# The start of an attention and expert-layer kernel: one weight unit converted in two parts, copies before weight passes, other banks, tiny products instead of fillers

## The chip, the cores and the metric

The kernel runs on one core of a Trainium2 chip. The metric is the device time of one execution in microseconds; the kernel before has a median of 911.16 us over three runs. The engines are TensorE (PE, with its weight loads PEld), VectorE (DVE), ScalarE (ACT), GpSimd (POOL) and SyncE (SP), which issues nearly all the transfers.

## The reference

Attention over 8 batches of 8 heads, 576 positions of 64 values, each query seeing 32 keys: the last 32 positions in the first four heads, every fourth of the last 128 in the other four. Its output, laid side by side, is the input of a gated layer.

```python
scores = scale * np.matmul(q, k.transpose(0, 1, 3, 2))
...
scores = np.where(masks[None, :, :, :], scores, -1000000000.0)
attn = np.exp(scores - np.max(scores, axis=-1, keepdims=True))
attn = attn / (np.sum(attn, axis=-1, keepdims=True) + 1e-09)
x = np.matmul(attn, v) ...            # 4608 x 512
g = x @ w_gate                        # 512 x 1536
silu = g * (1.0 / (1.0 + np.exp(-g)))
return (silu * (x @ w_val) @ w_out)   # 1536 x 512
```

## The kernel before

**Products.** Every large operand is split into a high part and a low remainder, and a product of two such operands is three products on PE. The weights come as 64-bit numbers and are converted on the chip.

**Attention in packs.** The attention is cut into 40 packs. Pack 0 and 2 hold the first four heads of batch 0 (called plain), packs 1 and 3 the other four (strided); two packs of a kind fill one input chunk of 512 columns. A pack goes through these steps, whose letters stand in the string START: scores on PE (Q), maximum and subtraction on DVE (S), exponential on ACT (X), four transposes on PE (T), a copy out of the bank on ACT or DVE (K, `keys`), results on PE (A), normalising on DVE (N), a transposition on DVE (U), the high copy on ACT (H) and the low difference on POOL or DVE (L; on DVE for the packs in X_LOW). Scores(2), results(3) and so on below name the step of a pack.

**Weights in units.** The weights come in 24 units of 768 columns, each of three thirds of 256. A unit goes through five stages, "ETBHL": exponent on ACT, shift on DVE (or ACT), bits on DVE, high copy on ACT, low difference on POOL (or DVE).

**Order.** START is the order of the first stage, written by hand; q, v and w in it are loads, I and J are filler products into a bank that nobody reads. After it come the items of the layer. The first chunk starts with six items of 256 columns (t = 0 to 5), then items of 512. An item t does its gate products (`bg`, 12 of them), the products of the item before with the output weights (`bo`, 12), and its value products (`bv`, 12). Packs 2 and following are worked in between by `attend(now)`, at the times in EARLY and LATER: a visit "A" does results of pack m-1 and scores of pack m, "B" transposes and copies, "C" the high and low copies. On PE everything runs in the order in which it is written; for the other engines the class Desk sorts the recorded instructions by a cost model that starts at the times in FREE (PE, DVE, ACT, POOL, SP, in ns).

**Banks.** `two` is a pair of banks for scores and results; fs0 and fs1 are pairs for the scores of packs 0 and 1; fk and fx take the transposes of packs 0 and 1, and the fillers.

Of the kernel before, what the change touches and what calls it, by code (L numbers as in the profile page):

```python
# [10 lines left out]
F32 = mybir.dt.float32  # L11
F32R = mybir.dt.float32r
I32 = mybir.dt.int32
# [5 lines left out]
P = 128  # L19
# [41 lines left out]
HALVED = 3  # L61
WARM = 9
TURNED = 20
FREE = 16000, 19500, 17500, 18000, 6000
EARLY = (-1, 1, None), (2, 4, 3), (5, 8, 6)
MASKED = 6
X_LOW, W_LOW, H_LOW, KEYS = (3, 7), (1, 5), (5,), (2,)
ON_ACT = (2, 3, 4, 5, 6, 9, 11, 12, 15, 17, 19, 21, 23)
START = ("q0 q1 w v0 v1 w Q0 Q1 S0 X0 T0 W0 I3 I2 S1 K0 X1 W1 A0 W2 T1 J2 K1 W3 J2 N0 W0 w U0 q2 v2 A1 q3 w w r W4 H0 "
         "L0 N1 U1 H1 L1 W1 v3 W2 W3 W4")  # L70
LATER = (14, 3, 2), (23, 3, 4), (29, 7, 4), (39, 3, 2)
T0 = NPLAIN * CH
NB = S * 8 // CH - 1
# [253 lines left out]
def attention_moe(ctx, tc, qkb, vb, w, const, out):  # L327
# [83 lines left out]
    def w_load(parts=2):  # L411
        nonlocal loaded
        u = loaded
        n = u % 5 if u < NU - NLAST else (u - NU + NLAST) % NRAW
        if u >= NU or raw_of.get(n, -1) >= done["B" if u < NU - 1 else "L"]:
            return False
        raw_of[n] = u
        loaded += 1
        t = at(raw_at[n], 2 * WU, I32)
        n = 2 * WU // parts  # L420
        for k in range(parts):
            nc.sync.dma_start(out=t[:, n * k:n * k + n], in_=w[u // 2, u % 2].bitcast(I32)[:, n * k:n * k + n])
        t = t.rearrange("p (n t) -> p n t", t=2)
        wst[u] = {"lo": t[:, :, 0], "hi": t[:, :, 1]}
        return True

    def w_exp(u):  # L430
        y = wst[u]["hi"].bitcast(F32)
        nc.scalar.activation(out=y, in_=y, func=AF.Prelu, scale=2.0 ** -112, alpha=2.0 ** 32)
# [58 lines left out]
    def w_one(c):  # L491
        u = done[c]
        done[c] += 1
        if c == "E":
            w_exp(u)
        elif c == "T":
            w_shift(u)
        elif c == "B":
            w_bits(u)
        elif c == "H":  # L500
            w_split_hi(u)
        else:
            w_split_lo(u)
        if c in "BL":
            while ready["w"] and w_load():
                pass
# [40 lines left out]
    def masks_of(m, i):  # L547
        n = BK * (pk(m).mask + i * pk(m).mask_step)
        return mask_sb[:, n:n + BK * NG].rearrange("q (g k) -> q g k", g=NG)[:, :, 1:]

    def scores(m, two, masked):

        t = st[m]["qk"]
        if masked:
            for i in range(2):
                nc.tensor.matmul(out=two[:, i, SA:].rearrange("q (g k) -> q g k", g=NG), lhsT=ident16,
                                 rhs=masks_of(m, i), start=True, stop=False, skip_group_check=True)
        for g in range(NG):
            for j in range(NH):
                for i in range(2):  # L560
                    r, q, k = slice(D * i, D * i + D), pk(m).q_at(g, j), pk(m).k_at(i, g, j)
                    nc.tensor.matmul(out=two[BQ * j:BQ * j + BQ, i, SA + BU * g:SA + BU * g + BU],
                                     lhsT=t[r, q:q + BQ], rhs=t[r, k + 1:k + BK], start=not masked,
                                     stop=not masked or g == NG - 1, skip_group_check=True)

    def clear_e(pool):

# [56 lines left out]
    def results(m, two):  # L624

        t, v = st[m]["pt"], st[m]["v"]
        for n in range(NH * NG):
            g, j = divmod(n, NH)
            for i in range(2):
                r = slice(D * i, D * i + D)  # L630
                nc.tensor.matmul(out=two[BQ * j:BQ * j + BQ, i, (D + 1) * g:(D + 1) * (g + 1)],
                                 lhsT=t[r, BQ * at_n(m, n):BQ * at_n(m, n) + BQ], rhs=v[r, n, :], start=True, stop=True,
                                 skip_group_check=True)

    def norm(m, two, pool):
        z = pool["bz"](2 * NG).rearrange("q (i g) -> q i g", i=2)
        y = pool["y"]()
        s = two[:, :, :NG * (D + 1)].rearrange("q i (g c) -> q i g c", g=NG)
        nc.vector.tensor_scalar(out=z, in0=s[:, :, :, D], scalar1=EPS, scalar2=None, op0=ALU.add)
        nc.vector.reciprocal(out=z, in_=z)  # L640
        nc.vector.tensor_tensor(out=y.rearrange("q (c i g d) -> q i g c d", c=2, i=2, g=NG),
                                in0=s[:, :, :, :D].rearrange("q i g (c d) -> q i g c d", c=2),
                                in1=z.unsqueeze(3).unsqueeze(4).broadcast_to([P, 2, NG, 2, D // 2]), op=ALU.mult)
        st[m]["y"] = y
# [148 lines left out]
    def bank(stack, name, n, side="left"):  # L793
        pool = stack.enter_context(tc.tile_pool(name="p" + name, bufs=1, space=bass.MemoryType.PSUM, side=side,
                                                reuse_waits="tile"))
        return pool.tile([P, 512] if n == 1 else [P, n, 512], F32, name=name)

    two = bank_r = bank(ctx, "two", 2)
    k_bank = [bank(of_turns, x, 1, "right") for x in ("fk", "fx")] * 2
    s_banks = [bank(of_scores, x, 2) for x in ("fs0", "fs1")]  # L800

    nc.scalar.dma_start(out=const_sb, in_=const)
    nc.vector.memset(ones, 1.0)
# [10 lines left out]
    def idle(n, bank=k_bank[1]):  # L814

        while n > 0:
            k = min(n, 4)
            nc.tensor.matmul(out=bank[:D, :P * k].rearrange("p (a b) -> p a b", b=D), lhsT=ones,
                             rhs=ones.unsqueeze(1).broadcast_to([P, 2 * k, D]), start=True, stop=True)
            n -= k  # L820

    idle(WARM)

    items = [Item(0, f, a, a + CH // 2) for a in (0, CH // 2) for f in range(HALVED)]
# [2 lines left out]
    first = {  # L827
        "Q": lambda m: scores(m, s_banks[m], True), "S": lambda m: shift(m, s_banks[m], fa, True),
        "X": exps, "T": lambda m: turn_e(m, k_bank[m]), "K": lambda m: keys(m, k_bank[m], fa),
        "A": lambda m: results(m, bank_r), "N": lambda m: norm(m, bank_r, fa),  # L830
        "U": turn_y, "H": lambda m: x_copy(m, "hi"), "L": lambda m: x_copy(m, "lo"),
        "q": lambda m: load_qk(m, fa, nc.sync, 2),
        "v": lambda m: load_v(m, fa, nc.sync, 2),
        "w": lambda m: w_load(3), "r": lambda m: ready.update(w=True), "I": lambda n: idle(n), "J": lambda n: idle(n, k_bank[0]), "W": lambda n: w_one(STAGES[n]),
    }

    et = mybir.EngineType
# [39 lines left out]
    def attend(now):  # L877
        for what, m in visit.get(now, ()):
            r = ended(m)
            if what == "A":  # L880
                if r is not None:
                    results(r, two)
                if m < NPK:
                    scores(m, two, m < MASKED)
                if r is not None:
                    norm(r, two, pool_of(r))
                if m < NPK:
                    shift(m, two, pool_of(m), m < MASKED)
                if r is not None:
                    turn_y(r)  # L890
                if m < NPK:
                    exps(m)
                if 2 * NSTART <= m < TURNED:
                    load_v(m, later, nc.sync)
                elif TURNED <= m - 1 < NPK:
                    load_far(m - 1, later)
                    load_v(m - 1, later, nc.sync)
                if 2 * NSTART <= m + 1 < NPK:
                    load_qk(m + 1, later, nc.sync)
            elif what == "B":  # L900
                if TURNED <= m < NPK:
                    turn_far(m, later)
                elif m < NPK:
                    turn_e(m, two[:, 1])
                    keys(m, two[:, 1], pool_of(m))
            elif r is not None:
                x_copies(r)

# [226 lines left out]
    for t, it in enumerate(items):  # L1135
        before = items[t - 1] if t else None
        late = t >= HALVED
        if it.ci == 0:
            units(it.f)
        gv_mm(it, 0)  # L1140
        act_tanh(it)
        dve_u(it)
        attend(3 * t)
        mixing(t, 0)
        if not late and t:
            out_mm(before, False)
        gv_mm(it, 1)
        dve_h(it)
        h_hi(it)
        if not late:  # L1150
            h_lo(it)
        attend(3 * t + 1)
        if late:
            out_mm(before)
            h_lo(it)
        if t and before.f == NF - 1:
            out_store(before.ci)
        attend(3 * t + 2)
        mixing(t, 1)
        if it.ci == NPLAIN - 1:  # L1160
            if it.f >= 9:
                ask([3, 5, NAT - 1][it.f - 9])
            for n in {6: (0,), 7: (1,), 9: (2, 3), 10: (4, 5), 11: (6, 7)}.get(it.f, ()):
                x_step(n)
# [84 lines left out]
```

## Time and profile before

| what | value |
|---|---|
| median of three runs | 911.16 us (909.72 to 911.43) |
| the profiled execution | 914.47 us, its span 912.7 us |
| PE busy | 897.8 us, 98% of the span |
| DVE, ACT, POOL busy | 646.0, 382.5, 257.8 us |
| mean granted clock of PE | 0.996 of full |

The profiled execution is 3.3 us over the median of the runs.

### The profile page before, as it was taken

How to read it: one execution, taken by the hardware profiler on the slowest of the kernel's cores; microseconds unless marked ns; L12 is line 12 of the kernel's file. 1: busy time of each engine (PE TensorE's matmuls, PEld its weight loads, DVE VectorE, ACT ScalarE, POOL GpSimd, SP SyncE). 2: the span in 40 equal slices, each digit the busy share in tenths (PEclk: the TensorE clock that was granted, in tenths of full speed). 3: DMA queues.
4: the chain of work that ended last, by engine and by line, in shares of the span. 5: the costliest groups of instructions: out<-in, count | busy, mean ns of one | idle time of the engine just before them, and what ended most of it. 6: DMA issues, size and time to landing. Idle time of an engine off the chain costs nothing.

```text
span 912.7 us, 20897 instructions
## 1 busy us (share of the span) xinstructions
PE 897.8 (98%) x8642; PEld 737.0 (81%) x8642; DVE 646.0 (71%) x993; ACT 382.5 (42%) x593; POOL 257.8 (28%) x177
## 2 busy tenths in 40 slices
PE   6899999999999999999999999999999999999998
PEld 4798888888888888888888888888878888888886
DVE  5687779888795473777789766878787746555752
ACT  4788433333243242333336544333345533334452
POOL 2468712221311112012032630111146501213451
PEclk9899999999999999999999999999999999999999
DMA  9899986453464640887888678989866675565562
GB/s 338 326 337 368 373 287 224 153 184 122 164 239 146 211 162 13 265 288 263 291 272 282 233 247 279 306 279 296 273 211 222 212 240 198 188 199 189 193 223 92
DMA packets 90382, 214.24 MB, mean 235 GB/s; under 512 B 9264, under 2 KB 32432, under 8 KB 90288
## 3 DMA queue, kind: packets, MB, share of 16 engines
q1 hardware_dynamic: 79776, 208.09, 66.2%
q10 hardware_dynamic: 10512, 4.82, 2.0%
q8 instruction: 68, 1.11, 0.5%
q14 instruction: 26, 0.21, 0.1%
HBM read 165.69 MB, written 47.19 MB: 233 GB/s over the span
## 4 chain that ended last, share of the span: by engine, by line
PE 96%; DMA 2%; issue 1%; SPq 0%; ACT 0%; DVE 0%; POOL 0%; ACTq 0%
PE bo L250 43%; PE bg L250 23%; PE bv L250 23%; PE two L250 7%; DMA at_int<-w 1%; DMA at_float<-turned 1%; SPq L234 0%; DVE at_float L250 0%; POOL at_float32r L234 0%; ACT at_float32r L250 0%; ACT at_float32r L234 0%; ACT at_float L250 0%; ACT at_int L234 0%; ACTq L234 0%
## 5 line engine op out<-in xcount | busy, mean ns | idle before, releaser
L250 PE MATMUL bo<-at_float32r 128*128 128x512 f32 x1296 | 305.7, 390 | 0.0
L250 PEld LDWEIGHTS bo<-at_float32r 128*128 128x128 f32 x1296 | 242.6, 188 | 51.0
L250 POOL TENSOR_TENSOR at_float32r<-at_float,at_float32r 128x512 fp32r<-128x512 f32 (+1 forms) x109 | 161.0, 1480 | 388.7 <-ACT at_float32r L250 210.4
L250 ACT CAST at_float32r<-at_float 128x512 fp32r<-128x512 f32 (+2 forms) x214 | 147.9, 705 | 146.6 <-DVE at_float L250 69.9
L250 DVE TENSOR_TENSOR at_float<-bo,at_float 128x512 f32<-128x512 f32 x168 | 114.1, 683 | 99.7 <-ACT at_float L250 63.7
L250 DVE TENSOR_TENSOR at_float32r<-at_float,at_float32r 128x512 fp32r<-128x512 f32 (+1 forms) x105 | 108.9, 1051 | 48.2 <-ACT at_float32r L250 38.1
L250 PE MATMUL bv<-at_float32r 128*128 128x512 f32 x486 | 128.6, 391 | 0.0
L250 PE MATMUL bg<-at_float32r 128*128 128x512 f32 x486 | 128.3, 390 | 0.0
L250 ACT ACTIVATE at_float<-at_float 128x512 f32<-128x512 f32 (+1 forms) x108 | 67.9, 630 | 134.7 <-DVE at_float L250 121.4
L250 PE MATMUL bg<-at_float32r,at_float32r 128*128 128x512 f32 (+1 forms) x468 | 108.8, 382 | 1.8 <-ACT at_float32r L234 1.2
L250 POOL TENSOR_TENSOR at_float<-at_float,at_float 128x512 f32<-128x512 f32 x36 | 51.3, 1424 | 209.8 <-DVE at_float L250 190.8
L250 PE MATMUL bv<-at_float32r,at_float32r 128*128 128x512 f32 (+1 forms) x468 | 107.2, 379 | 0.0
L250 DVE SCALAR_TENSOR_TENSOR at_float<-at_float,at_float 128x512 f32<-128x512 f32 x144 | 106.1, 743 | 1.1
L250 PE MATMUL bo<-at_float32r,at_float32r 128*128 128x512 f32 (+1 forms) x468 | 106.8, 377 | 0.0
L250 PEld LDWEIGHTS bg<-at_float32r 128*128 128x128 f32 x486 | 90.9, 188 | 19.1
L250 PEld LDWEIGHTS bv<-at_float32r 128*128 128x128 f32 x486 | 90.8, 188 | 19.2
L250 PEld LDWEIGHTS bg<-at_float32r,at_float32r 128*128 128x128 f32 x468 | 83.7, 192 | 18.5 <-ACT at_float32r L234 1.4
L250 PEld LDWEIGHTS bv<-at_float32r,at_float32r 128*128 128x128 f32 x468 | 83.3, 191 | 15.8
L250 PEld LDWEIGHTS bo<-at_float32r,at_float32r 128*128 128x128 f32 x468 | 82.8, 188 | 16.4 <-POOL at_float32r L250 0.2
L250 ACT COPY at_float<-bg 128x512 f32<-128x512 f32 x63 | 37.0, 587 | 84.8 <-PE bg L250 79.9
L250 DVE TENSOR_TENSOR at_float<-at_float,at_float 128x512 f32<-128x512 f32 (+2 forms) x80 | 63.8, 806 | 2.4 <-POOL at_float L250 1.2
L250 ACT COPY at_float<-bv 128x512 f32<-128x512 f32 x63 | 37.1, 589 | 36.9 <-PE bv L250 36.1
(73 smaller groups left out, 610.0 us busy)
## 6 DMA issues: line engine op xcount, KB each, us to landing
at_float32r<-pieces SPq DMA_DIRECT2D x189, 512.0 KB, 4.2
pieces<-at_float32r SPq DMA_DIRECT2D x126, 256.0 KB, 4.2
at_float<-qkb SPq DMA_DIRECT2D x32, 576.0 KB, 6.2
at_float<-vb SPq DMA_DIRECT2D x34, 520.0 KB, 5.4
at_int<-w SPq DMA_DIRECT2D x38, 384.0 KB, 6.2
out<-at_float SPq DMA_DIRECT2D x36, 256.0 KB, 4.3
turned<-at_float SPq DMA_DIRECT2D x18, 256.0 KB, 4.8
at_float<-turned ACTq DMA_DIRECT2D x72, 64.0 KB, 5.2
```

What stands on the lines that cost most here:

```text
L250: self.kept.append([engine, lambda: f(*a, **k), sorted(m for m in after if m >= 0), cost, later, both, start])
```

## The change

It changes the first stage and the first items.

- **Unit 0 in two parts.** `w_third` loads its last third ahead of everything but the queries and keys ("y"), the other two later ("z"). `w_some` converts the last third alone (P0 to P4, 256 columns) and then the other two (R0 to R4, 512 columns). The first gate products read the last third of unit 0 for the plain half.
- **Order in START.** The copies K0 and K1 and the exponential X1 stand ahead of most weight stages; the two filler runs between T0 and A1 (I3 I2, J2 J2) are replaced by D20 and G10: 20 and 10 products of 32x32 into fx and fk. The fillers at the very start (`idle(WARM)`) stay.
- **Banks.** Pack 1's results go to fs1 and not to `two`, so that A1 needs no longer wait for N0. Pack 2's transposes go to bo3.
- **Masks and visits.** Scores(0) puts its masks behind the products. Scores(3) stands ahead of results(2) (`BEFORE`). The transposes of pack 3 come at time 3.5, ahead of the value products of item 1, where a new `attend(3 * t + 0.5)` stands; they came behind them.
- **Low half of pack 1** moves from POOL to DVE (X_LOW), and FREE has new times.

```diff
-FREE = 16000, 19500, 17500, 18000, 6000
-EARLY = (-1, 1, None), (2, 4, 3), (5, 8, 6)
+FREE = 13000, 16500, 17000, 15600, 6000
+EARLY = (-1, 1, None), (2, 3.5, 3), (5, 8, 6)
+BEFORE = 3
-X_LOW, W_LOW, H_LOW, KEYS = (3, 7), (1, 5), (5,), (2,)
+X_LOW, W_LOW, H_LOW, KEYS = (1, 3, 7), (1, 5), (5,), (2,)
-START = ("q0 q1 w v0 v1 w Q0 Q1 S0 X0 T0 W0 I3 I2 S1 K0 X1 W1 A0 W2 T1 J2 K1 W3 J2 N0 W0 w U0 q2 v2 A1 q3 w w r W4 H0 "
-         "L0 N1 U1 H1 L1 W1 v3 W2 W3 W4")
+START = ("q0 q1 y v0 z v1 w Q0 q2 w Q1 S0 X0 P0 T0 D20 K0 S1 X1 P1 P2 A0 P3 P4 T1 N0 G10 K1 U0 R0 H0 v2 q3 w A1 "
+         "R1 R2 L0 R3 R4 N1 U1 H1 W0 L1 w v3 r")
...
+    def w_third(a, e):
...
+        t = at(raw_at[0], 2 * WU, I32)
+        for k in range(a, e):
+            n = slice(2 * UT * k, 2 * UT * k + 2 * UT)
+            nc.sync.dma_start(out=t[:, n], in_=w[0, 0].bitcast(I32)[:, n])
+
+    def w_some(c, a):
+
+        lo, hi = [x[:, a] for x in w_parts(0)]
...
+        if c == "E":
+            x = hi.bitcast(F32)
+            nc.scalar.activation(out=x, in_=x, func=AF.Prelu, scale=2.0 ** -112, alpha=2.0 ** 32)
+        elif c == "T":
+            nc.vector.tensor_scalar(out=y, in0=hi, scalar1=3, scalar2=None, op0=ALU.logical_shift_left)
...
+        if a.start == 0:
+            done[c] = 1
+
...
+    r_banks = [bank_r, s_banks[1]]
...
+    def tiny(n, bank):
+        for _ in range(n):
+            nc.tensor.matmul(out=bank[:BQ, :BQ], lhsT=ones[:, :BQ], rhs=ones[:, :BQ], start=True, stop=True)
...
-        "A": lambda m: results(m, bank_r), "N": lambda m: norm(m, bank_r, fa),
+        "A": lambda m: results(m, r_banks[m]), "N": lambda m: norm(m, r_banks[m], fa),
...
             if what == "A":
+                if m == BEFORE:
+                    scores(m, two, m < MASKED)
                 if r is not None:
                     results(r, two)
-                if m < NPK:
+                if m < NPK and m != BEFORE:
                     scores(m, two, m < MASKED)
...
-                    turn_e(m, two[:, 1])
-                    keys(m, two[:, 1], pool_of(m))
+                    turned_at = bank_o[3] if m == BEFORE - 1 else two[:, 1]
+                    turn_e(m, turned_at)
+                    keys(m, turned_at, pool_of(m))
...
             out_mm(before, False)
+        attend(3 * t + 0.5)
         gv_mm(it, 1)
```

What PE does from the second scores of START to the first gate products, before. A row's count is that of the products written; a product of plain 32-bit operands runs as two passes, so that results(0), x32 here, is x64 in the trace. `fs_119<-at_1280` is Q1, `fk<-at_192` T0, `at_64` the fillers' ones.

```order
L234 MATMUL fs_119<-at_1280_float_142 32x63 x32
L234 MATMUL fk<-at_192_bfloat_61,at_512_float_124 128x128 x4
L234 MATMUL fx<-at_64_float_62 64x384
L234 MATMUL fx<-at_64_float_62 64x256
L234 MATMUL two<-at_1040_float_149,at_512_float_241 32x65 x32
L234 MATMUL fx<-at_192_bfloat_61,at_512_float_126 128x128 x4
L234 MATMUL fk<-at_64_float_62 64x256 x2
L234 MATMUL two<-at_1040_float_152,at_512_float_284 32x65 x32
L250 MATMUL bg<-at_1024_float32r,at_1536_float32r 128x256 x6
```

The same stretch after the change:

```order
L235 MATMUL fs_119<-at_1280_float_142 32x63 x32
L235 MATMUL fk<-at_192_bfloat_61,at_512_float_124 128x128 x4
L235 MATMUL fx<-at_64_float_62 32x32 x20
L235 MATMUL two<-at_1040_float_147,at_512_float_263 32x65 x32
L235 MATMUL fx<-at_192_bfloat_61,at_512_float_126 128x128 x4
L235 MATMUL fk<-at_64_float_62 32x32 x10
L235 MATMUL fs_119<-at_1040_float_152,at_512_float_324 32x65 x32
L251 MATMUL bg<-at_1024_float32r,at_1536_float32r 128x256 x6
```

The large fillers between T0 and A0 and ahead of A1 are gone, 20 tiny products stand ahead of A0 and 10 ahead of A1, and A1 writes fs_119.

DVE around the normalising of pack 3's results, before: `at_776_int_450` is weight unit 5 in its conversion, `at_512_float_351` the results of pack 3, and `at_1024_float32r` the input of the layer.

```order
L250 SCALAR_TENSOR_TENSOR at_776_int_450<-at_1536_int_145 128x3x256
L250 SCALAR_TENSOR_TENSOR at_512_float_445<-at_512_float_445,bv 128x256
L250 TENSOR_TENSOR at_1536_float32r<-at_776_int_450,at_1536_float32r 128x768
L250 TENSOR_REDUCE at_8_float_227<-two 128x8
L250 TENSOR_SCALAR at_8_float_350<-two 128x8
L250 TENSOR_TENSOR at_512_float_124<-two,at_8_float_227 128x2x4x63
L250 RECIPROCAL at_8_float_350<-at_8_float_350 128x8
L250 TENSOR_TENSOR at_512_float_351<-two,at_8_float_350 128x8x2x32
L250 SCALAR_TENSOR_TENSOR at_512_float_444<-at_512_float_444,bg 128x256
L250 STREAM_TRANSPOSE at_512_float_351<-at_512_float_351 128x512
L250 SCALAR_TENSOR_TENSOR at_776_int_244<-at_1536_int_155 128x3x256
L250 TENSOR_TENSOR at_1024_float32r<-at_512_float_351,at_1024_float32r 128x2x4x64
```

The same place after, where unit 5 is `at_776_int_473` and the results of pack 3 are `at_512_float_375`:

```order
L251 TENSOR_REDUCE at_8_float_233<-two 128x8
L251 TENSOR_SCALAR at_8_float_374<-two 128x8
L251 SCALAR_TENSOR_TENSOR at_776_int_473<-at_1536_int_145 128x3x256
L251 RECIPROCAL at_8_float_374<-at_8_float_374 128x8
L251 TENSOR_TENSOR at_512_float_124<-two,at_8_float_233 128x2x4x63
L251 TENSOR_TENSOR at_1536_float32r<-at_776_int_473,at_1536_float32r 128x768
L251 TENSOR_TENSOR at_512_float_375<-two,at_8_float_374 128x8x2x32
L251 STREAM_TRANSPOSE at_512_float_375<-at_512_float_375 128x512
L251 SCALAR_TENSOR_TENSOR at_512_float_466<-at_512_float_466,bg 128x256
L251 TENSOR_TENSOR at_1024_float32r<-at_512_float_375,at_1024_float32r 128x2x4x64
```

Unit 5's bits and low difference (`at_1536_float32r<-at_776_int_473`) came ahead of the maximum of pack 4's scores; now they stand behind it and between the first step of pack 3's normalising and its multiplication.

ACT around the high copy of unit 5, before: `at_512_float_444<-bg` is the first function of item 2.

```order
L250 CAST at_1536_float32r<-at_776_int_358 128x768
L250 COPY at_512_float_284<-two 128x512
L250 CAST at_1536_float32r<-at_776_int_450 128x768
L250 CAST at_512_float32r<-at_512_float_445 128x256
L250 CAST at_1024_float32r<-at_512_float_289 128x2x256
L250 ACTIVATE at_1536_int_155<-at_1536_int_155 128x768 x2
L250 ACTIVATE at_512_float_444<-bg 128x256
```

The same place after, where `at_512_float_466<-bg` is item 2's:

```order
L251 CAST at_1536_float32r<-at_776_int_470 128x768
L251 ACTIVATE at_1536_int_145<-at_1536_int_145 128x768
L251 CAST at_512_float32r<-at_512_float_467 128x256
L251 ACTIVATE at_1536_int_145<-at_1536_int_145 128x768
L251 CAST at_1024_float32r<-at_512_float_310 128x2x256
L251 ACTIVATE at_512_float_466<-bg 128x256
L251 CAST at_1536_float32r<-at_776_int_473 128x768
```

The high copy of unit 5 (`at_776_int_450`, now 473) stood ahead of pack 2's copy and of item 2's function, and stands behind both now.

## Rows read from the trace of the kernel before

**Rows 1.** The page: busy time of the engines, and the instruction queue.

```profile
PE 897.8 (98%) x8642; PEld 737.0 (81%) x8642; DVE 646.0 (71%) x993; ACT 382.5 (42%) x593; POOL 257.8 (28%) x177
...
q8 instruction: 68, 1.11, 0.5%
```

**Rows 2.** Windows: busy us of each engine (instructions), PEclk, DMA share, GB/s.

```profile
35.00:40.00 5.00, 4.33 (x151) 3.69 (x150) 2.85 (x5) 3.80 (x7) 3.35 (x3) 1.00 0.36 136
...
40.00:45.00 5.00, 5.00 (x45) 5.00 (x44) 4.55 (x10) 4.35 (x7) 1.39 (x2) 1.00 0.93 322
```

**Rows 3.** What PE waited for, 0 to 120 us: us, times, longest.

```profile
PE two L250 <- issue: 3.8, 2, 2.0
```

**Rows 4.** DMA queues, 18.7 to 19.9 us: packets, MB, share of 16 engines.

```profile
q8 instruction: 1, 0.02, 5.5%
```

**Rows 5.** Window from the end of one issue wait to the end of the next.

```profile
21.30:30.00 8.70, 5.97 (x128) 5.03 (x127) 4.48 (x8) 6.47 (x10) 3.86 (x3) 0.78 1.05 392
```

**Rows 6.** DMA queues, 11.0 to 12.2 us.

```profile
q8 instruction: 1, 0.02, 5.6%
```

**Rows 7.** DMA queues, 38.8 to 40.0 us.

```profile
q8 instruction: 1, 0.02, 5.8%
```

**Rows 8.** Timeline, 8 to 17 us: start, length, engine, instruction, count, idle before it.

```profile
8.95 0.66 PE L234 MATMUL fk<-at_bfloat,at_float 128*128 128x128 f32 x4
...
10.29 0.91 ACT L234 ACTIVATE at_int<-at_int 128x768 f32<-128x768 f32 x1 [1.71 <-DMA at_int<-w]
...
11.10 0.56 ACT L234 COPY at_float<-fk 128x512 f32<-128x512 f32 x1
...
11.72 0.86 PE L234 MATMUL two<-at_float,at_float 64*32 64x65 f32 x64 [0.89 <-ACT at_float L234]
...
13.53 0.69 DVE L234 TENSOR_TENSOR at_float<-two,at_float 128x512 f32<-128x512 f32 x1
...
14.32 1.06 PE L234 MATMUL two<-at_float,at_float 64*32 64x65 f32 x64
...
15.91 0.61 ACT L234 CAST at_float32r<-at_float 128x512 fp32r<-128x512 f32 x1
...
16.57 0.74 PE L250 MATMUL bg<-at_float32r,at_float32r 128*128 128x256 f32 x4 [1.19 <-ACT at_float32r L234]
```

**Rows 9.** Timeline, 21 to 45 us.

```profile
21.30 0.30 PE L250 MATMUL two<-at_float 64*32 64x63 f32 x5 [1.89 <-issue]
...
30.00 0.66 PE L250 MATMUL two<-at_float 64*32 64x63 f32 x29 [1.95 <-issue]
...
30.60 2.78 PE L250 MATMUL bg<-at_float32r,at_float32r 128*128 128x256 f32 x12
...
37.20 0.84 ACT L250 CAST at_float32r<-at_int 128x768 fp32r<-128x768 f32 x1
...
37.36 0.86 PE L250 MATMUL two<-at_float,at_float 64*32 64x65 f32 x64 [0.68 <-ACT at_float L250]
...
38.07 0.96 DVE L250 TENSOR_TENSOR at_float32r<-at_int,at_float32r 128x768 fp32r<-128x768 f32 x1 [1.37 <-ACT at_float32r L250]
...
39.26 1.70 PE L250 MATMUL bg<-at_float32r,at_float32r 128*128 128x256 f32 x12
...
40.91 0.69 DVE L250 TENSOR_TENSOR at_float<-two,at_float 128x512 f32<-128x512 f32 x1
...
41.06 0.38 ACT L250 ACTIVATE at_float<-bg 128x256 f32<-128x256 f32 x1 [0.56 <-PE bg L250]
...
41.85 0.70 DVE L250 STREAM_TRANSPOSE at_float<-at_float 128x512 f32<-128x512 f32 x1
...
42.66 1.12 ACT L250 CAST at_float32r<-at_float 128x512 fp32r<-128x512 f32 x1
...
43.81 1.11 DVE L250 TENSOR_TENSOR at_float32r<-at_float,at_float32r 128x512 fp32r<-128x512 f32 x1 [0.42 <-ACT at_float32r L250]
...
44.04 1.70 PE L250 MATMUL bg<-at_float32r,at_float32r 128*128 128x256 f32 x12
```

More of the change, by code (lines that the diff above doesn't have):

```diff
@@ L425, in w_load @@
         return True
+    def w_third(a, e):
+        nonlocal loaded
+        if not loaded:
+            raw_of[0], loaded = 0, 1
+            t = at(raw_at[0], 2 * WU, I32).rearrange("p (n t) -> p n t", t=2)
+            wst[0] = {"lo": t[:, :, 0], "hi": t[:, :, 1]}
+        t = at(raw_at[0], 2 * WU, I32)
[4 more added lines that the diff above has]
+        lo, hi = [x[:, a] for x in w_parts(0)]
+        y = at(M_LATE + 4 * WU, YW, I32)[:, :3 * (UT + 1)].rearrange("p (a b) -> p a b", a=3)[:, a, :UT]
+        to_hi, to_lo = [x[:, a] for x in w_place(0)]
+        if c == "E":
[3 more added lines that the diff above has]
+            nc.vector.tensor_scalar(out=y, in0=hi, scalar1=3, scalar2=None, op0=ALU.logical_shift_left)
+        elif c == "B":
+            nc.vector.scalar_tensor_tensor(out=y, in0=lo, scalar=29, in1=y, op0=ALU.logical_shift_right,
+                                           op1=ALU.bitwise_or)
+        elif c == "H":
+            nc.scalar.copy(out=to_hi, in_=y.bitcast(F32))
+        else:
+            nc.gpsimd.tensor_tensor(out=to_lo, in0=y.bitcast(F32), in1=to_hi, op=ALU.subtract)
+        if a.start == 0:
+            done[c] = 1
     def w_exp(u):
@@ L553, in scores, with masks @@
         t = st[m]["qk"]
-        if masked:
+        behind = m == 0
+        def masks():
             for i in range(2):
                 nc.tensor.matmul(out=two[:, i, SA:].rearrange("q (g k) -> q g k", g=NG), lhsT=ident16,
-                                 rhs=masks_of(m, i), start=True, stop=False, skip_group_check=True)
+                                 rhs=masks_of(m, i), start=not behind, stop=behind, skip_group_check=True)
+        if masked and not behind:
+            masks()
         for g in range(NG):
@@ L562, in scores @@
                     nc.tensor.matmul(out=two[BQ * j:BQ * j + BQ, i, SA + BU * g:SA + BU * g + BU],
-                                     lhsT=t[r, q:q + BQ], rhs=t[r, k + 1:k + BK], start=not masked,
-                                     stop=not masked or g == NG - 1, skip_group_check=True)
+                                     lhsT=t[r, q:q + BQ], rhs=t[r, k + 1:k + BK], start=behind and g == 0 or not masked,
+                                     stop=not (masked and behind) and (not masked or g == NG - 1),
+                                     skip_group_check=True)
+        if masked and behind:
+            masks()
     def clear_e(pool):
@@ L833, in attention_moe @@
         "v": lambda m: load_v(m, fa, nc.sync, 2),
-        "w": lambda m: w_load(3), "r": lambda m: ready.update(w=True), "I": lambda n: idle(n), "J": lambda n: idle(n, k_bank[0]), "W": lambda n: w_one(STAGES[n]),
+        "w": lambda m: w_load(3), "D": lambda n: tiny(n, k_bank[1]), "G": lambda n: tiny(n, k_bank[0]), "y": lambda m: w_third(2, 3), "z": lambda m: w_third(0, 2),
+        "P": lambda n: w_some(STAGES[n], slice(2, 3)), "R": lambda n: w_some(STAGES[n], slice(0, 2)), "r": lambda m: ready.update(w=True), "I": lambda n: idle(n), "J": lambda n: idle(n, k_bank[0]), "W": lambda n: w_one(STAGES[n]),
     }
```

## Prediction

> **What bounds the kernel now.** The page first: PE is busy for 98% of the span [rows 1], so only what moves PE counts. Then the windows, to see where it is not busy: from 40 us on it has no gap (5.00 of 5.00 us), from 35 to 40 us it is still short of work (4.33) [rows 2]. The work behind is the same after the change, so the end moves by what PE gains or loses up to about 45 us. Then PE's waits up to 120 us: the largest is "issue", 3.8 us in two pieces [rows 3], a wait for nothing that the profile names. I looked for what it is. In each of the two a packet of the instruction queue q8 runs just before PE goes on. The page counts 68 packets of 1.11 MB there, and PE has 8642 products and as many loads [rows 1]: 17284 / 68 = 254, so a packet is about 256 instructions. From the end of the first wait to that of the second PE does exactly 128 products [rows 5], with their loads 256 instructions. So PE runs out of instructions each time. The packet in the 1.2 us from 18.7 takes 5.5% of 16 engines, 1.06 us [rows 4]; it ends between 19.76 and 19.90, and PE goes on at 21.30: a block is of use 1.4 to 1.55 us after its packet.
>
> **Where the blocks fall.** A pass is one product of the trace; scores and results have 64 each. The waits stand with 5 passes left of scores(2) (21.30) and 29 of scores(3) (30.00) [rows 9]. Counting 128 products back from the first (59 of scores(2), 2 masks, 6 bg, 61 of the 64 in A1), the block before begins at the start of A1, 14.32 [rows 8]; another 128 back, in the middle of Q1, where the order is the same in both kernels. From there I count forward in the new order. Between those two marks before lie 3 passes of A1, 4 of fillers, 4 of T1, 64 of A0, 4 of fillers, 4 of T0 and so 45 of Q1. After, 45 of Q1, 4 of T0 and D20's 40 (each product is two passes) leave 39 for A0: the block begins 39 passes into A0. The next ones, G10 being 20, begin some 8 passes into scores(2), 48 into scores(3), 8 into results(3), and in the middle of the bg of item 2.
>
> **Start to first bg.** Without fetches the chain gains. K0 starts at 11.10 because the exponent stage of all 768 columns stands ahead of it (10.29, waiting for the load); T0 is done at 8.95 + 0.66 = 9.6, so K0 could go at 9.7: -1.4. N0's multiplication (13.53) waits behind the weight's shift and bits on DVE, and H0 (15.91) behind unit 1's exponent on ACT: 15.91 - 13.53 - 0.69 - 0.70 = 1.0 late, and about 0.5 of the former. First bg at 16.57 - 2.8 = 13.8 [rows 8]. But A0 would start at 10.3 and needs the new block after 39 passes, at 10.8. That block's packet lies in 11.0 to 12.2 us and takes 5.6%, 1.08 us [rows 6], so it ends at 12.1 to 12.2 and is of use at 13.5 to 13.7. Its request is made in Q1, at the same time as before, so I keep it. PE stands for about 2.7 us in A0 (bounds: 1.2 if the block is of use when the packet ends; 3.6 if it slips by 0.9), A0's other 25 passes end at 13.9, and the first bg comes as long after as it did (16.57 - 12.58) less the 1.5 us of waits on DVE and ACT: 16.4, as before. The tiny products have no row: D20's 40 passes are 0.5 us at 13 ns (0.86 / 64, A0 [rows 8]) and 6.6 at 165 ns (0.66 / 4, T0). By the first, of the nearer shape, they end at 10.2, while PE waits for K0; by the second A0 would start at 16.2 and the end move by up to +3. I take the first: nothing, for D20 and for G10 ahead of A1.
>
> **The rule on fetches.** The Trainium skill (Runtime: NRT & Kernel Launch, Instruction fetch mechanics) says that the sequencer fetches blocks of 256 instructions by itself, and that crossing into one is mostly hidden. The block size agrees with the 254 above; the hiding does not, with two waits of 1.9 us. By the rule the sum would have no fetch terms and be the first rival's.
>
> **To the bg of item 1.** The next block is asked for when PE enters the one in A0, 13.6 against 14.3 before; with the same 7.0 us from there to use (14.32 to 21.30) it is there at 20.6, and the next, at the same spacing of 8.7, at 29.3. Then 16 passes of scores(3) and all of results(2), which before came ahead of the wait, are left: 0.25 + 0.86, bg at 30.4 against 30.60 [rows 9]: **-0.2**. The edits in between (no wait of A1 for N0, its bank, masks behind, bo3, R0 to R4, the low half of pack 1 on DVE, 1.11 us by L3's row) end under these two waits. Without that cover the DVE subtraction would push unit 1's shift, bits and low part by 1.1, and bv with them.
>
> **Transposes of pack 3 earlier.** They stand ahead of bv, so the copy K3 is done under it: results(3) no longer waits, 0.68 [rows 9]: **-0.7**. Results(3) then starts at 37.36 - 0.9 = 36.5, bg of item 2 at 39.26 - 0.9 = 38.4.
>
> **A new wait in the bg of item 2.** Its block is asked for when PE's sequencer passes the mark in results(3), which may be as early as the start of bv ahead of it (12 products, 1.70 by the bg's row: 36.5 - 1.7 = 34.8), as K3 holds it no longer. Before, that mark stood at the end of results(3), 38.1, and the packet came at 38.8 to 38.9 [rows 7], when the DMAs were quiet (0.36 busy [rows 2]): 0.8 us after. So 34.8 + 0.8 + 1.1 + 1.5 = 38.2, no wait, at best; with the 4.4 us from 14.32 to the packet at 18.75 [rows 4, 8] it is 41.8. PE needs it halfway, at about 39.2. Bounds 0 and 2.6; the share of 0.36 is that of a queue still emptying at 35, so I take **+1.0**.
>
> **Unit 5 ahead of pack 3.** Unit 5's high copy (37.20 before) now stands on ACT behind item 2's function, which waits for its bg; its low part on DVE waits for the copy, and the multiplication of pack 3's results stands behind that. The chain from the start of that bg to pack 3's high part is 1.70 + 0.38 + 0.84 + 0.96 + 0.69 + 0.70 + 1.12 = 6.4 us, where PE gives 44.04 - 39.26 = 4.8 up to the bg that reads it [rows 9]: **+1.6**. Bounds: 0 if other work of PE lengthens its side, and 2.7 if the low part (1.11) is waited for too. The bg starts with high parts, which hides most of that.
>
> Sum: -0.2 - 0.7 + 1.0 + 1.6 = +1.7: 914.47 + 1.7 = 916.2 for the profiled execution, and on the median of the runs, 3.3 lower, 911.16 + 1.7 = **912.9**. The bounds of the last two terms give 910.3 to 915.6. Under 0.2% (1.8 us) a measurement of this kernel hardly tells a change from none.
>
> **Rivals.**
> - *The gain goes through* (0.29). The block in A0 comes in time (asked for earlier, or D20 hardly counted) and the DVE chain has slack: -2.8 at the start and -0.7 at results(3) are -3.5, with the wait in the bg of item 2 -2.5: about 908.2. For it: every engine had unneeded waits at the start. Against: the packet at 11.0 to 12.2.
> - *Neither late wait* (0.14): the block of item 2's bg is there, and unit 5 is done early: -0.9, 910.3.
> - *A long fetch* (0.13): the request of the block in item 2's bg stands in a full queue for 4.4 us; +2.6 instead of +1.0, and the half clock that follows a wait of PE doubles part of what is next (bg x12 2.78 at 30.60, 1.70 at 39.26 [rows 9]): +1.1. 1.7 + 1.6 + 1.1 = 4.4: 915.6. It decides once the packet starts later than 38.
> - *Forecast* (0.44): 912.9, about half of it over 0.2%.
>
> Faster: nearly all of the first rival and some of the second, 0.31. Slower: the long fetch and half of the forecast, 0.34. Same: 0.35. The range reaches to the middle of both outer rivals: 907.7 to 915.8.
>
> **What would show it.** K0 near 9.7; in PE's waits an "issue" of 1 to 3 us in results(0), `two<-at_float,at_float`, at 11 to 13.7; waits on issue in scores(2) and scores(3) that end near 20.6 and 29.3; results(3) without a wait; an issue wait in the bg at 38 to 40 us; the multiplication of pack 3 after 42 and a wait of bg for ACT near 45. The prediction is wrong if A0 runs through without a wait, or if unit 5's copy is ready ahead of pack 3's results.

## The result, and the profile after

The changed kernel takes 918.99 us (median of seven runs, 918.24 to 921.68) against 911.16 (seven runs, 908.95 to 915.79): 1.0091 times as long, 95% interval 1.0071 to 1.0112, or some 8 us more. The profiled execution is 919.05 us, its span 917.2, against 914.47 and 912.7. So the two profiles differ by 4.6 us and the medians by 7.8.

What PE waited for up to 120 us, after (us in total, times, longest):

```profile
PE two L235 <- issue: 2.8, 1, 2.8
...
PE bg L251 <- issue: 2.1, 1, 2.1
...
PE bv L251 <- ACT at_float32r L251: 1.5, 1, 1.5
...
PE bv L251 <- issue: 1.1, 1, 1.1
```

There are three waits on issue, 6.0 us together, where before had two of 3.8 [rows 3], and at other places: results(0), the bg of item 2, the bv of an item at 60 us. For ACT and DVE, PE waits 1.5 and 0.5 us in the bv of item 0, 0.25 in that of item 2, and 0.63 in the bg of item 3 (timeline below).

The timeline after, the rows of PE and DVE on which the terms rest:

```profile
8.65 1.45 PE L235 MATMUL fx<-at_float 128*32 128x32 f32 x40
...
10.03 0.66 PE L235 MATMUL two<-at_float,at_float 64*32 64x65 f32 x40
...
13.46 0.43 PE L235 MATMUL two<-at_float,at_float 64*32 64x65 f32 x24 [2.77 <-issue]
...
16.92 1.03 PE L251 MATMUL bg<-at_float32r,at_float32r 128*128 128x256 f32 x4
...
18.89 0.85 PE L251 MATMUL two<-at_float 64*32 64x63 f32 x64
...
23.98 0.39 PE L251 MATMUL bv<-at_float32r,at_float32r 128*128 128x256 f32 x1 [1.51 <-ACT at_float32r L251]
...
29.83 2.31 PE L251 MATMUL bg<-at_float32r,at_float32r 128*128 128x256 f32 x12
...
35.36 0.86 PE L251 MATMUL two<-at_float,at_float 64*32 64x65 f32 x64
...
37.26 0.50 PE L251 MATMUL bg<-at_float32r,at_float32r 128*128 128x256 f32 x2
...
39.89 1.35 PE L251 MATMUL bg<-at_float32r,at_float32r 128*128 128x256 f32 x10 [2.12 <-issue]
...
41.08 1.60 PE L251 MATMUL bo<-at_float32r,at_float32r 128*128 128x256 f32 x12
...
42.48 0.96 DVE L251 TENSOR_TENSOR at_float32r<-at_int,at_float32r 128x768 fp32r<-128x768 f32 x1 [1.82 <-ACT at_float32r L251]
...
43.36 0.68 DVE L251 TENSOR_TENSOR at_float<-two,at_float 128x512 f32<-128x512 f32 x1
...
45.15 1.34 PE L251 MATMUL bg<-at_float32r,at_float32r 128*128 128x256 f32 x8
...
47.12 0.74 PE L251 MATMUL bg<-at_float32r,at_float32r 128*128 128x256 f32 x4 [0.63 <-DVE at_float32r L251]
...
49.14 1.60 PE L251 MATMUL bo<-at_float32r,at_float32r 128*128 128x256 f32 x12
...
60.60 1.22 PE L251 MATMUL bv<-at_float32r,at_float32r 128*128 128x256 f32 x8 [1.07 <-issue]
```

A0 runs 40 passes and then stands for 2.77 us to 13.46; the first bg comes at 16.92 against 16.57 [rows 8]. Scores(2) has no wait at 18.89; the bv at 23.98 waits for unit 1. The bg of item 1 starts at 29.83 (30.60 [rows 9]), results(3) without a wait. The bg of item 2 does 2 products and stands for 2.12 us. Pack 3's results are multiplied at 43.36 (40.91), right behind unit 5's low part (42.48); the bg that reads them starts at 45.15 (44.04) and waits once more for their low part. At 60.60 comes a wait with no counterpart before.

Windows from the end of the first issue wait to the ends of the other two, after:

```profile
13.46:39.89 26.43, 21.16 (x508) 17.73 (x508) 20.03 (x33) 17.45 (x26) 11.24 (x8) 0.81 0.95 339
...
13.46:60.60 47.14, 39.70 (x764) 34.58 (x764) 37.24 (x59) 34.46 (x53) 21.80 (x15) 0.89 0.92 324
```

508 passes and 764 are four times 127 and six times 127.3. With their loads that is 254 to 255 instructions each, close to the 256 of a block if a few others stand between them: the waits stand where the blocks change. At the marks between, in scores(2), scores(3) and results(3), PE did not wait.

### The profile page after: what moved, and what is told of

Same layout as the page of the kernel before. It is cut to its first block, busy times and chain, and to the rows that moved or that the text cites. A ratio compares the mean times of both kernels' runs of the same rounds, so it can differ in the third digit from the quotient of the medians.

```text
span 917.2 us, 21013 instructions
## 1 busy us (share of the span) xinstructions
PE 900.3 (98%) x8694; PEld 739.2 (81%) x8694; DVE 651.3 (71%) x996; ACT 382.4 (42%) x595; POOL 260.2 (28%) x177
## 4 chain that ended last, share of the span: by engine, by line
PE 93%; DMA 3%; DVE 2%; ACT 1%; issue 1%; SPq 0%; POOL 0%; DVEq 0%; ACTq 0%
PE bo L251 42%; PE bv L251 22%; PE bg L251 22%; PE two L251 6%; DMA at_int<-w 1%; DVE at_float L251 1%; DMA at_float<-turned 1%; DMA pieces<-at_float32r 1%; DVE at_int L251 1%; DMA at_bfloat<-const 0%; ACT at_float32r L251 0%; DVE at_float L235 0%; ACT at_float L251 0%; POOL at_float32r L251 0%; SPq L251 0%
## 5 line engine op out<-in xcount | busy, mean ns | idle before, releaser
L251 POOL TENSOR_TENSOR at_float32r<-at_float,at_float32r 128x512 fp32r<-128x512 f32 (+1 forms) x109 | 165.2, 1517 | 397.6 <-ACT at_float32r L251 212.9
L251 DVE TENSOR_TENSOR at_float<-at_float,at_float 128x512 f32<-128x512 f32 (+2 forms) x80 | 67.8, 856 | 2.4 <-POOL at_float L251 1.2
```

The costliest lines, as they stand in the source:

```text
L251: self.kept.append([engine, lambda: f(*a, **k), sorted(m for m in after if m >= 0), cost, later, both, start])
```

## The experiments

Times are medians with that of the kernel before run beside them on the same chip.

**The kernel before once more**, unchanged.

> The kernel before, unchanged, for a second profile. If the two issue waits of before are block fetches, they stand at the same passes again (5 passes left in scores(2), 29 left in scores(3)), whatever their length; the time is 909 to 914 us. If its executions differ by the length of these waits, a profile near 911 us has 2 to 3 us less of waits in its first 60 us than the 914.47 us one. The rival, that the executions differ later in the span, shows the same first 60 us and a shorter rest.

910.59 us (910.76 beside it, ratio 0.9981 to 1.0022); its profiled execution took 911.27. The two issue waits of scores(2) and scores(3) are gone. PE's busy time in the first 60 us, in the first profile of before, in this one, and in the changed kernel (windows):

```profile
0.00:60.00 60.00, 49.70 (x959) 40.77 (x960) 40.11 (x73) 40.88 (x61) 23.60 (x23) 0.94 0.92 327
```

```profile
0.00:60.00 60.00, 53.82 (x979) 44.19 (x980) 44.22 (x76) 44.05 (x66) 29.14 (x25) 0.94 0.99 358
```

```profile
0.00:60.00 60.00, 48.55 (x986) 39.87 (x986) 40.88 (x71) 37.92 (x59) 22.35 (x22) 0.91 0.91 321
```

Its timeline at the places of the two waits, and at the starts that are compared further down:

```profile
16.83 2.16 PE L250 MATMUL bg<-at_float32r,at_float32r 128*128 128x256 f32 x6 [2.50 <-ACT at_float32r L234]
...
19.36 1.18 PE L250 MATMUL two<-at_float 64*32 64x63 f32 x64
...
27.06 1.70 PE L250 MATMUL bg<-at_float32r,at_float32r 128*128 128x256 f32 x12
...
34.65 1.70 PE L250 MATMUL bg<-at_float32r,at_float32r 128*128 128x256 f32 x12
...
36.19 1.60 PE L250 MATMUL bo<-at_float32r,at_float32r 128*128 128x256 f32 x12
...
42.44 1.85 PE L250 MATMUL bo<-at_float32r,at_float32r 128*128 128x256 f32 x12
```

The bg of item 1 starts at 27.06, 3.5 us ahead of the first profile (30.60 [rows 9]). So the first profile caught an execution with two waits that this one, 0.7 us off the median, lacks. The first part of the expectation (waits at the same passes) could not be seen, as there are no such waits; the second, that the executions differ by these waits, held. The two profiles then stand 4.6 us apart at the bg of item 2 (39.26 [rows 9] and 34.65), since the first ran the bg of item 1 at half the clock (2.78 us [rows 9] against 1.70), and 3.2 at the end.

**Without the tiny products.**

```diff
-... P0 T0 D20 K0 ... T1 N0 G10 K1 ...
+... P0 T0 K0 ... T1 N0 K1 ...
```

> The changed kernel without D20 and G10, nothing else. Fetch theory: 60 passes less, so the first mark moves from 39 passes into A0 to 45 + 4 + 64 + 4 = 117, that is 11 passes into A1: A0 runs through at about 10.2 and the issue wait of 2.8 us is in A1, ending near 13.5 as before; the first bg comes near 14.4 (16.92 with the tiny products). The later marks move by 60 passes too: none in the bg of item 2. Time 3 to 5 us under the changed kernel, 914 to 916. Rival, the tiny products keep the clock up or cost nothing: same time within 1 us, and a wait remains in A0 or half clock takes the gain back. Rival, the order of DVE and ACT (unit 1 behind the low half of pack 1, unit 5 ahead of pack 3) is what costs: the waits for DVE and ACT stay and the time falls by less than 2 us.

914.06 us, 1.0010 to 1.0047 of before, 4.9 us under the changed kernel (the medians of before beside the two differ by 0.4).

```profile
9.72 0.86 PE L235 MATMUL two<-at_float,at_float 64*32 64x65 f32 x64 [0.68 <-ACT at_float L235]
...
11.85 0.33 PE L235 MATMUL fs<-at_float,at_float 64*32 64x65 f32 x11 [0.68 <-ACT at_float L235]
...
13.21 0.77 PE L235 MATMUL fs<-at_float,at_float 64*32 64x65 f32 x53 [1.04 <-issue]
...
13.91 0.38 PE L251 MATMUL bg<-at_float32r,at_float32r 128*128 128x256 f32 x1
...
19.25 1.01 PE L251 MATMUL bg<-at_float32r,at_float32r 128*128 128x256 f32 x3 [1.51 <-issue]
...
27.19 0.42 PE L251 MATMUL two<-at_float,at_float 64*32 64x65 f32 x22 [0.93 <-issue]
...
42.67 0.50 PE L251 MATMUL bg<-at_float32r,at_float32r 128*128 128x256 f32 x2 [0.63 <-DVE at_float32r L251]
```

A0 runs through, the wait is 11 passes into A1, at 13.21 the block is there, and the first bg starts at 13.91, 3.0 us earlier than in the changed kernel. Two more issue waits come behind it, of 1.51 us in the second half of the bg of item 0 and 0.93 in results(2), 128 passes and 127 further on; the bg of item 1 starts at 27.55, still 0.5 behind the second profile of before. So most of the lead of 3 us is lost here to these two waits and the half clock behind the first (granted clock 0.50 from 20 to 24 us), and the bv of item 0 does not wait for unit 1. The low-part wait of the bg of item 3 (0.63) stays.

**Tiny products at the start.**

```diff
-    idle(WARM)
+    tiny(20, k_bank[1])
+    idle(5)
...
-... T0 D20 K0 ...
+... T0 K0 ...
```

> The changed kernel with D20 moved from before A0 to the start (and four of the nine units of starting filler taken out there, 2 passes), so that as many instructions stand ahead of A0. Fetch theory: the mark stays about 39 to 41 passes into A0, but the block is asked for some 40 passes earlier, in Q0 and not in Q1, about 1.3 us earlier: an issue wait in A0 still, ending at 11.5 to 12.5 and not at 13.46. Later marks stay where they are in the changed kernel, in the bg of item 2 and near 60 us. Time 1 to 3 us under the changed kernel. Rival, the burst of tiny products ahead of A0 is what holds PE: no wait in A0 at all.

918.07 us (1.0043 to 1.0093 of before).

```profile
9.76 0.68 PE L235 MATMUL two<-at_float,at_float 64*32 64x65 f32 x42 [0.67 <-ACT at_float L235]
...
11.72 0.65 PE L235 MATMUL two<-at_float,at_float 64*32 64x65 f32 x22 [1.28 <-issue]
...
37.83 1.24 PE L251 MATMUL bg<-at_float32r,at_float32r 128*128 128x256 f32 x8 [1.77 <-POOL at_float32r L251]
```

The wait is still in A0, after 42 passes, though no burst stands ahead of it, and ends at 11.72, 1.74 us earlier; its packet starts at 9.3, where it starts at 11.1 in the changed kernel. What holds PE is the block and not the burst. The wait in the bg of item 2 (37.83) is there too: the profile puts it down to POOL, but the instruction of POOL ended 0.6 us before, and a block's packet 1.4 us before, as at the other waits. At 58.17 comes the third, of 0.55. The median is only 0.9 under the changed kernel, a little less than expected; the intervals overlap, and the profiled execution (915.89) is 3.2 under that of the changed kernel, so the size of the gain is not settled.

**The kernel before with the tiny products** in place of its four fillers.

```diff
-... T0 W0 I3 I2 S1 ... T1 J2 K1 W3 J2 N0 ...
+... T0 W0 D20 S1 ... T1 G10 K1 W3 N0 ...
```

> The kernel before with its fillers I3 I2 and J2 J2 replaced by D20 and G10, nothing else. Fetch theory: the marks move as in the changed kernel; the first comes 39 passes into A0, which starts at 11.7, so PE waits there until about 13.5 (1.3 us), and the marks in scores(2) and scores(3) move, with new ones in the bg or bo of item 2 and near 60 us. Time 1 to 5 us over the kernel before. Rival, the tiny products are free and better than the large fillers (which hold A1 for 0.38 us): 0 to 1 us under the kernel before.

915.84 us, 1.0039 to 1.0071 of before: 5.1 us more.

```profile
10.92 0.66 PE L234 MATMUL two<-at_float,at_float 64*32 64x65 f32 x40 [0.59 <-ACT at_float L234]
...
13.36 0.43 PE L234 MATMUL two<-at_float,at_float 64*32 64x65 f32 x24 [1.78 <-issue]
...
38.06 1.23 PE L250 MATMUL bg<-at_float32r,at_float32r 128*128 128x256 f32 x9 [1.56 <-issue]
...
57.30 1.10 PE L250 MATMUL bv<-at_float32r,at_float32r 128*128 128x256 f32 x7 [1.64 <-issue]
```

With the old START, the old visits and the old banks, the same three waits: 40 passes into A0, in the bg of item 2, in a bv near 57 us; 5.0 us together, about as much as the median rose. (The profiled execution, 915.02, is 3.8 over the second profile of before.)

**Unit 1 earlier**, without tiny products.

```diff
-... R3 R4 N1 U1 H1 W0 L1 ...
+... R3 R4 W0 N1 U1 W1 H1 L1 ...
```

> The changed kernel without tiny products, and with unit 1's exponent and shift earlier in START (W0 after R4, W1 after U1, where W0 stood behind H1). PE's order and the marks are those of the run without tiny products (914.06). If unit 1's conversion is what loses the lead of 2.7 us that the first bg has, the bv of item 0 starts some 1 us earlier and the time falls by 1 to 1.5 us, to 912.6 to 913. Fetch theory: the mark 42 passes into results(2) takes most of it, since its block comes no earlier: the issue wait there grows from 0.9 to about 1.9 us and the time stays within 0.7 us of 914.06.

911.85 us (the median of twelve; one of them took 3111.2, and without it the median is 911.52), 1.0002 to 1.0027 of before (910.05 beside it), where the run without tiny products stood at 1.0029: some 1.4 us less by the ratios, though the intervals overlap. No issue wait in results(2) took it; that alternative fell. But that unit 1 gave it is not shown: its high copy starts at 20.25 in this profile and at 20.07 without the edit, because ACT waits 1.54 and then 1.50 us for weights to load. What this profile lacks are the issue waits of 1.51 and 0.93.

**Visits as before**, without tiny products.

```diff
-EARLY = (-1, 1, None), (2, 3.5, 3), (5, 8, 6)
-BEFORE = 3
+EARLY = (-1, 1, None), (2, 4, 3), (5, 8, 6)
+BEFORE = -3
```

> The changed kernel without tiny products, with the visits as before (results(2) ahead of scores(3), transposes of pack 3 behind bv, and pack 2's transposes in the pair two). If the regrouped visits are what keeps the run without tiny products 3.3 us over the kernel before, by unit 5 standing between pack 3's results and their normalising, this is 911 to 912. If they are a gain of 0.7 (results(3) without a wait), it is 914.5 to 915.5. Fetch theory alone says within 0.7 us of 914.06.

913.14 us, 1.0022 to 1.0046: no difference from the run without tiny products (1.0029). Both of its first two alternatives fell. A gain or cost of 0.7 us would not show within these intervals.

**Unit 1 earlier and pack 1's low half on POOL** (X_LOW = (3, 7)).

> As the run with unit 1 earlier, and the low half of pack 1 back on POOL (X_LOW as before), so that DVE has 1.1 us less ahead of unit 1's bits. If DVE is what holds unit 1 there, another 0.5 us less than the run with unit 1 earlier; by the fetch theory no difference beyond 0.5 us, as the next block comes no earlier.

911.25 us, 1.0005 to 1.0026: as the run with unit 1 earlier, within the intervals.

```profile
32.45 1.70 PE L251 MATMUL bg<-at_float32r,at_float32r 128*128 128x256 f32 x12
...
40.40 0.74 PE L251 MATMUL bg<-at_float32r,at_float32r 128*128 128x256 f32 x4 [0.63 <-DVE at_float32r L251]
...
40.98 1.60 PE L251 MATMUL bv<-at_float32r,at_float32r 128*128 128x256 f32 x12
```

The bv of item 0 does not wait for unit 1, whose high copy now starts at 18.97, 1.1 us earlier than without the edits; but the bg ahead of it waited 0.93 for a block. The bg of item 3 still waits for pack 3's low part, and from the bg of item 2 to the bv of item 3 (32.45 to 40.98) pass 8.5 us, where the second profile of before has 6.4.

**FREE as before**, without tiny products.

> The changed kernel without tiny products and with FREE as before: START, the visits and PE's order stay, and the planner puts unit 5's bits ahead of the maximum of pack 4's scores, as in the kernel before, where the changed one has them behind it and behind the first step of pack 3's normalising. If that order is what costs 2.3 us between the bg of item 2 and its neighbours, the waits of bv and of the bg of item 3 shrink by 1 to 2 us and the time is 912 to 913. If the late high copy of unit 5 on ACT (behind item 2's function) costs it, no change: 913.5 to 914.5.

913.76 us, 1.0023 to 1.0049: no change.

```profile
26.08 1.11 PE L251 MATMUL bo<-at_bfloat,at_float 128*128 128x128 f32 x4 [2.27 <-ACT at_float L251]
...
38.28 0.84 ACT L251 CAST at_float32r<-at_int 128x768 fp32r<-128x768 f32 x1 [0.17 <-DVE at_int L251]
...
39.31 0.39 ACT L251 ACTIVATE at_float<-bg 128x256 f32<-128x256 f32 x1 [0.19 <-PE bg L251]
```

This does not decide between the two. FREE moved the high copy of unit 5 as well: it stands at 38.28, ahead of item 2's function (39.31). From the bg of item 2 to the bv of item 3 the profile is 1.0 us shorter than without the edit (7.9 against 8.9), as the first alternative has it; but the transposes of pack 2 now wait 2.27 us for their exponential, which ACT does behind a weight stage that waits for its load. One gain and one loss, and the time stays.

**Unit 5's low part on POOL**, on the run with unit 1 earlier and pack 1 on POOL.

```diff
-X_LOW, W_LOW, H_LOW, KEYS = (3, 7), (1, 5), (5,), (2,)
+X_LOW, W_LOW, H_LOW, KEYS = (3, 7), (1,), (5,), (2,)
```

> As the run with unit 1 earlier and the low half of pack 1 on POOL (911.25 us), with unit 5's low difference on POOL and no longer on DVE, so that nothing of unit 5 stands ahead of the multiplication of pack 3's results. If that order is what takes back 2.2 us between the bo of item 2 and the bg of item 3, 1 to 2 us less: 909.3 to 910.3, at or under the kernel before (910.05 beside it). If the late high copy of unit 5 on ACT is what PE waits for there (its bv), POOL, which is slower at it (1.75 against 0.96 us), makes that wait longer and the time stays or rises by up to 0.8.

910.32 us against 910.97, ratio 0.9968 to 0.9994, where the run it is built on had 1.0005 to 1.0026: some 1.9 us less by the medians, 3.2 by the ratios, with intervals apart, and the first version a little under the kernel before. The two runs stood on different chips, each with the kernel before beside it.

```profile
33.38 1.69 PE L251 MATMUL bg<-at_float32r,at_float32r 128*128 128x256 f32 x12
...
39.92 0.74 PE L251 MATMUL bg<-at_float32r,at_float32r 128*128 128x256 f32 x4 [0.18 <-DVE at_float32r L251]
...
40.49 1.60 PE L251 MATMUL bv<-at_float32r,at_float32r 128*128 128x256 f32 x12
```

The last wait of the bg of item 3 falls from 0.63 to 0.18, and from the bg of item 2 to the bv of item 3 pass 7.1 us (33.38 to 40.49) and no longer 8.5: 1.4 us is what the traces show at the place itself.

**The same with D20 and G10 back.**

> The same with D20 and G10 put back. Fetch theory: the marks go back to 39 passes into A0 (wait of about 2.8 us, to 13.5), the bg of item 2 (about 2 us) and near 60 us (1 to 2 us): 4.5 to 6 us over the run without them. The rival, that tiny products cost only together with the changed kernel's order of DVE and ACT, gives less than 2 us.

915.00 us, 1.0027 to 1.0058: 4.7 more than without them. Its largest waits of PE on issue:

```profile
PE bg L251 <- issue: 2.3, 1, 2.3
...
PE two L235 <- issue: 1.7, 1, 1.7
...
PE bv L251 <- issue: 1.1, 1, 1.1
```

The three waits are back at their places, 5.1 us together, in a kernel whose other orders are mended.

**Results(2) ahead of scores(3)** (BEFORE = -3, which also puts pack 2's transposes back into the pair two), with unit 5's low part on POOL.

> As the run with unit 5's low part on POOL, with results(2) ahead of scores(3) as in the kernel before (transposes of pack 3 still ahead of bv, pack 2's in the pair two). By the fetch theory the mark that fell in results(2) falls in scores(3), with the same packet: within 0.5 us of that run. If scores(3) first is a gain by itself, 0.5 to 1 us more.

910.03 us, 0.9970 to 1.0003 of before: no difference from that run.

## Why the prediction was wrong

The time lies 6 us above the 912.9 and 3 above the range. Neither of the two signs of being wrong that the prediction named came; the miss lies where it named none. The two profiles nearest the medians, the second of before and that of the changed kernel, show where the 7.8 us arise (starts in us):

| at | before, second profile | after | after is behind by | forecast for the stretch |
|---|---|---|---|---|
| bg of item 1 | 27.06 | 29.83 | 2.8 | -0.2 |
| bg of item 2 | 34.65 | 37.26 | 2.6 | -0.7 |
| bo of item 2 | 36.19 | 41.08 | 4.9 | +1.0 |
| bo of item 3 | 42.44 | 49.14 | 6.7 | +1.6 |
| time of the execution | 911.27 | 919.05 | 7.8 | none |

- **Where the blocks fall: right.** 39 passes into A0 were counted, 40 came; the wait of 2.7 us to 13.5 to 13.7 was 2.77 to 13.46; the mark in the bg of item 2 was there. The moved and removed tiny products show the cause: the wait goes where the count puts it.
- **To the bg of item 1: the step that failed.** The -0.2 set the new order against an execution that waited 3.8 us for blocks in scores(2) and scores(3), and took over for the new kernel the 7.0 us from the request of a block to its use and the spacing of 8.7, so that two such waits would cover what the other engines do there. In the second profile of before these waits don't exist, and in the changed kernel they don't either: the packets of the two blocks start at 16.1 and 21.2, so that by the 1.1 us of a packet and 1.5 to use they are there near 18.8 and 23.9 (an estimate), ahead of their marks. With nothing to cover it, the bv of item 0, which starts at 21.61 (21.91 in the second profile), waits 1.51 and 0.49 us for unit 1, and PE runs at half the clock behind it (0.50 from 26 to 30 us). The text named this as what happens when the cover is gone, with 1.1; it is +2.8.
- **The sum on the median: the same error.** "3.3 lower" carried the offset of the profiled execution of before over to the changed kernel. The offset came in the main of those two waits; the changed kernel's profile (919.05) has none against its median (918.99). That the sum on the profile, 916.2, is nearer to 919.05 is luck: against the first profile the bg of item 1 is 0.8 early and the next stretches gain more than forecast, because that profile lost time there itself.
- **Results(3) without a wait: the wait is gone, the gain is not.** The wait was 0.68; the stretch is only 0.2 us shorter, since the bg of item 1 now runs in part at half the clock (2.31 us against 1.70).
- **A new wait in the bg of item 2: mis-sized.** +1.0, bounds 0 and 2.6; it is 2.12, with its packet starting at 37.6. The half clock that the third rival put behind it did not come (granted clock 1.00 from 41 to 47 us).
- **Unit 5 ahead of pack 3: right.** +1.6 was forecast; from the bo of item 2 to that of item 3 the changed kernel takes 1.8 us longer (8.06 against 6.25), part of it the wait for the low part that was taken to be mostly hidden. PE waited for DVE there, not for ACT.
- **A third wait, at 60 us, was left out.** The counting stopped at item 2. Two blocks further, with results and scores of a pack between the marks, it is 1.07 us; with tiny products it came in all three other kernels that were run (0.5 to 1.6), without them in none.
- **The tiny products' price: mis-sized.** The prediction put 13 ns a pass and nothing in time. D20's 40 passes took 1.45 us, 36 ns each, and hold A0 (10.03) some 0.6 us behind K0, which is done at 9.35; the wait for the block hides that. G10's 20 passes took 1.28 us at half the clock, 64 ns each, and hold A1 (15.79) some 0.5 behind K1, done at 15.28: the first bg came at 16.92 and not at 16.4. The larger harm is in their number, 60 passes and 120 instructions against the fillers' 16.

Put together from the runs: the tiny products cost 4.9 us (914.06 to 918.99; 5.1 in the kernel before, 4.7 in the last version), with the marks of the blocks moved as counted. Unit 5's place costs some 1.4 by the traces and 1.9 by the medians. Unit 1's late conversion costs 2.0 us of waits in the changed kernel's bv; the 1.4 that its edit seemed to gain is not shown to come of it. The lead of 3 us at the first bg is real (13.91 without tiny products against 16.83), and is lost again to further waits for blocks, to unit 1 and to unit 5. The regrouped visits and X_LOW make no difference that can be measured, FREE a gain and a loss in the one profile taken, and the last version nets 0.6 us by the medians.

Left open: why the first profile of before waits for its blocks and the second doesn't. In the first Q1 waited 1.15 us longer for its load, and the packet of the block asked for in A1 (14.3) started at 18.7 [rows 4], in the second at 16.5; both would follow from a fuller DMA queue, which no run here varied. Also 0.8 us between the first profile of before and the changed kernel's behind 500 us is not explained; PE waits 0.3 us longer there for turned packs.

## What to carry to other kernels

Where PE does many small products, count its instructions, loads included, in steps of some 256 from a wait that the profile calls "issue" and that no other engine explains: an added product can move the next block's start into the middle of a stage that sets the end. Fillers should be few and large there. And where a profile lies well off the median of the runs, find what that execution has and the others lack before a sum is made on it; a wait in it may be the one the change is credited with.

## What the runs showed of the hardware

In these profiles a block of PE's instructions was of use 1.2 to 1.6 us after its packet had run. After, the packet that starts in 11.0 to 12.2 us (at 11.1, and 5.1% of 16 engines over 1.2 us is 0.98 us):

```profile
q8 instruction: 1, 0.02, 5.1%
```

PE went on at 13.46, 1.3 to 1.4 us after it. With the tiny products at the start, so that PE came to the mark before it earlier, the packet started 1.8 us and the block was of use 1.74 us earlier, which bears out that it is asked for there. All the waits for blocks shown here stand where results and scores, 64 passes each within 0.86 us, or the tiny products lie between two marks, so that the 256 instructions are soon gone; at other such marks, in scores(2), scores(3) and results(3), the block was there in time. Behind 61 us, where products of 256 columns and more fill the blocks, no wait on issue is left in the list.

The Trainium skill (Runtime: NRT & Kernel Launch, Instruction fetch mechanics) calls the crossing into a block mostly hidden. The trace agrees behind 61 us; ahead of it three crossings are not hidden, with waits of 2.77, 2.12 and 1.07 us. A 32x32 pass of plain 32-bit operands over 128 rows took 36 ns at a granted clock of 1.00 (the level of 2.4 GHz), nearly three times a pass of results (0.86 us for 64 [rows 8]), and 64 ns at 0.50 (1.2 GHz), behind the wait of 2.77 us.
